# Moving fill work between score halves, warm-up matmuls and norms in an attention-plus-MLP kernel

## The chip, the cores and the metric

The kernel runs on one core of a Trainium2 chip. The metric is device microseconds of one execution. TensorE (PE) multiplies matrices into PSUM, VectorE (DVE), ScalarE (ACT) and GpSimd (POOL) do the element-wise work, and SyncE (SP) issues most DMAs. Each engine works through its own instructions in order and waits on semaphores for the others.

## The reference

`S` is 2048 tokens, `D` 512, 32 heads of 16, `F` 1376. `LN` is a layer norm without weights.

```python
xn = LN(x)
q, k, v = split(xn @ wqkv)                   # 32 heads x 16
# every token attends to itself and to 7 earlier tokens, 2 apart
logits = q . k[pos - 2*w] * 16**-0.5, w = 0..7 (masked where pos - 2*w < 0)
s = softmax(logits) @ v, then @ wo
h  = gelu(LN(xn) @ w1)
hs = concat(4 column groups of h, shifted by +1, -1, +2, -2 tokens) @ w2
x1 = xn + hs
g  = silu(x1 + gelu(LN(x1) @ w3) @ w4)
out = x + s * g
```

## The kernel before

Tokens are split into two parities `p` (even and odd), 1024 tokens each, so that a window of 8 tokens 2 apart becomes a window of 8 neighbours. A chunk `c` (0 to 3) is 512 tokens of one parity. The order of the instructions on every engine is written out by hand: the calls from line 684 on emit them in order, each engine takes its own.

Stages, in order:

1. **Start (L159 to L702).** 16 warm-up matmuls on ones (L161). The four 128-token tiles of chunk 0 go one by one through statistics (`ln_first`, L298 to L302: DVE statistics, then a `pow(-0.5)` on POOL), normalisation on DVE (`first_n`, L306), transposes on TensorE and an ACT copy (`first_t`, L314, L315). The first q/k projections (`qk_pair`, L391) follow on halves of the chunk. `mask_cols`, `mask_rows`, `mask_wide`, `mask_turn` and `mask_fill` build a banded penalty that is put beside q and k as extra rows of the contraction.
2. **Projections and first MLP layer (L703 to L763).** For each chunk: statistics (`ln_stats`, L275, L276, and `rsqrt_eps` on POOL, L267, L268), norm (`ln_norm`, L322), transposes (`stage_t`), q/k projection (`qk_pair`, ACT copy L398). The second layer norm of a row that is normalised already is only a factor per token: `ln_again` computes it on POOL (L331, L332, and `rsqrt_eps`), `stage_d` puts it on a diagonal (DVE, L361), `stage_r` spreads it over partitions with one matmul (L368) and an ACT copy (L369), `stage_m` multiplies (DVE, L375). `stage_w1` has 2 x 4 matmuls (L420) and a GELU on ACT. `spread` moves q and k by DMA from SP.
3. **First phase: attends 0 to 8 (even tokens).** 1024 tokens make 9 units (128, then 120 each, 56 at the end). An attend `n` (L836) emits: scores of the first half of the heads (`scores`, L553: 16 small matmuls, 8 into each of two PSUM tiles, tags `s` and `t`, each followed by an exp on ACT, L558); the weighted sum of the attend before (L576); the fill of list `a`; the values of the next unit (L533, copied by DVE, L537); scores of the second half; the fill of list `b`; then the `late` list. The tags `s` and `t` have one buffer each, so a half's matmuls wait for the exps of the half before. Fill is one of `w2_tile` ("w": 4 matmuls L443 and a DVE add L447) and `qk_one` ("q": 4 matmuls L407 and an ACT copy L412). Both and the values take turns in two PSUM banks (tags `w`, `b`). The strings at L776 say which fill goes where.
4. **w3 (L861 on).** 88 x 2 matmuls (L487) with GELUs (L492), and in between the last weighted sum of the first phase, layer norms and loads.
5. **Second phase: attends 9 to 17 (odd tokens).** Here the weighted sum also stands behind the first half, and the values behind the second. The fill is a `w4_tile` (11 matmuls, L507, and a DVE add, L513), split 5 into list `a` and 6 into list `b`; two attends have three `final_tile`s in its place. `gate(t)` follows a finished w4 tile: tanh on ACT (L522) and a product on DVE (L523).
6. **Tail (L893 on).** w4 tiles 8 to 15, each followed by a `final_tile`: 4 matmuls with `wo` (L663), a product on DVE (L671) directly from PSUM or, with `act=True`, after an ACT copy (L670), and an add (L673) on the engine that is passed. The last three tiles (5, 6, 7) have their adds on DVE; the store of the last one is issued by ACT.

Of the kernel before, what the change touches and what calls it, by code (L numbers as in the profile page):

```python
# [9 lines left out]
ALU = mybir.AluOpType  # L10
# [5 lines left out]
def kernel(  # L16
# [14 lines left out]
    nc = tc.nc  # L31
# [8 lines left out]
    NF = (F + P - 1) // P  # L40
    FL = F - (NF - 1) * P
    EPS = 1e-5
# [72 lines left out]
    def psa(name):  # L115
        cnt["p"] += 1
        return pst("sto"[cnt["p"] % 3], name)
# [6 lines left out]
    for c in range(NCH):  # L124
        p, k = c // 2, c % 2
        n = 1 if c == 0 else 2
        for t0 in range(k * TPC, (k + 1) * TPC, n):
            nc.sync.dma_start(
                out=xn[p][:, t0 : t0 + n, :],
# [26 lines left out]
    nhalf = const.tile([P, TPC], F32, name="nhalf")  # L156
    nc.vector.memset(nhalf[:], -0.5)

    wm = psa("warm_ps")  # L159
    for i in range(16):  # L160
        nc.tensor.matmul(  # L161
            wm[:, i % 2, :], lhsT=ones_bf[:], rhs=ones_bf.unsqueeze(1).to_broadcast([P, TPC, P]),
            start=True, stop=True,
        )
# [101 lines left out]
    def rsqrt_eps(dst, var):  # L266
        nc.gpsimd.tensor_scalar(out=dst, in0=var, scalar1=EPS, scalar2=None, op0=ALU.add)  # L267
        nc.gpsimd.tensor_tensor(out=dst, in0=dst, in1=nhalf[:, 0 : dst.shape[-1]], op=ALU.pow)  # L268

    def layer_stats(src, name, lo=0, hi=TPC):  # L270
        n = hi - lo
        st = small.tile([P, n, nc.vector.BN_STATS_DIM], F32, name=name + "s", tag=f"{name}s{n}", bufs=2)
        mv = small.tile([P, n, nc.vector.BN_AGGR_DIM], F32, name=name + "m", tag=f"{name}m{n}", bufs=8 if n == 1 else 4)
        for j in range(n):
            nc.vector.bn_stats(out=st[:, j, :], in_=src[:, lo + j, :])  # L275
            nc.vector.bn_aggr(out=mv[:, j, :], in_=st[:, j, :])  # L276
        rstd = small.tile([P, n], F32, name=name + "r", tag=f"{name}r{n}", bufs=8 if n == 1 else 4)
        rsqrt_eps(rstd, mv[:, :, 1])
        return mv, rstd
# [5 lines left out]
    def ln_stats(c, lo=0, hi=TPC):  # L285
        p, k = c // 2, c % 2
        lns.setdefault(c, []).append((lo, hi, *layer_stats(xn[p][:, k * TPC : (k + 1) * TPC, :], "l1", lo, hi)))
# [3 lines left out]
    def ln_first(j):  # L291
        if not first:
            first["st"] = small.tile([P, TPC, nc.vector.BN_STATS_DIM], F32, name="l0s", tag="l0s", bufs=1)
            first["mv"] = small.tile([P, TPC, nc.vector.BN_AGGR_DIM], F32, name="l0m", tag="l0m", bufs=1)
            first["r"] = small.tile([P, TPC], F32, name="l0r", tag="l0r", bufs=1)
            lns[0] = [(0, TPC, first["mv"], first["r"])]
        st, mv, rstd = first["st"], first["mv"], first["r"]
        nc.vector.bn_stats(out=st[:, j, :], in_=xn[0][:, j, :])  # L298
        nc.vector.bn_aggr(out=mv[:, j, :], in_=st[:, j, :])
        r = rstd[:, j : j + 1]  # L300
        nc.vector.tensor_scalar(out=r, in0=mv[:, j, 1:2], scalar1=EPS, scalar2=None, op0=ALU.add)
        nc.gpsimd.tensor_tensor(out=r, in0=r, in1=nhalf[:, 0:1], op=ALU.pow)  # L302

    def first_n(j):
        mv, rstd = first["mv"], first["r"]
        nc.vector.tensor_scalar(  # L306
            out=xn[0][:, j, :], in0=xn[0][:, j, :], scalar1=mv[:, j, 0:1],
            scalar2=rstd[:, j : j + 1], op0=ALU.subtract, op1=ALU.mult,
        )

    def first_t(j):
        pt = pst("wb"[j % 2], "tr_ps").bitcast(BF16)[:, 0, 0:CH].rearrange("p (a q) -> p a q", a=ND)
        for dt in range(ND):
            nc.tensor.transpose(pt[:, dt, :], xn[0][:, j, dt * P : (dt + 1) * P], ident[:])  # L314
        nc.scalar.copy(out=xnT[0][:, :, j * P : (j + 1) * P], in_=pt)  # L315

    def ln_norm(c):
        p, k = c // 2, c % 2
        x_c = xn[p][:, k * TPC : (k + 1) * TPC, :]
        for lo, hi, mv, rstd in lns[c]:  # L320
            for j in range(lo, hi):
                nc.vector.tensor_scalar(  # L322
                    out=x_c[:, j, :], in0=x_c[:, j, :], scalar1=mv[:, j - lo, 0:1],
                    scalar2=rstd[:, j - lo : j - lo + 1], op0=ALU.subtract, op1=ALU.mult,
                )

    def ln_again(c):
        r2 = small.tile([P, TPC], F32, name="r2", tag="r2")
        for lo, hi, mv, rstd in lns[c]:
            r = r2[:, lo:hi]  # L330
            nc.gpsimd.tensor_tensor(out=r, in0=rstd, in1=rstd, op=ALU.mult)  # L331
            nc.gpsimd.tensor_tensor(out=r, in0=r, in1=mv[:, :, 1], op=ALU.mult)  # L332
        rsqrt_eps(r2, r2)
        r2s[c] = r2

    def stage_t(c, h):
# [29 lines left out]
    def stage_r(c):  # L366
        rp = psb("rrep_ps")
        nc.tensor.matmul(rp, lhsT=ones_bf[:], rhs=dgs.pop(c).rearrange("p j q -> p (j q)"), start=True, stop=True)  # L368
        nc.scalar.copy(out=xn2T[c][:, ND - 1, :], in_=rp)  # L369
# [41 lines left out]
        dst, n0 = qk_dst(p, nt)  # L411
        nc.scalar.copy(out=dst[:, n0, cs], in_=pt)  # L412

    def stage_w1(c, a):
        p, k = c // 2, c % 2
        pt = psa("w1_ps")
        for b in range(2):
            g = 2 * a + b
            for dt in range(ND):
                nc.tensor.matmul(  # L420
                    pt[:, b, :], lhsT=w1_sb[:, dt, g * P : (g + 1) * P], rhs=xn2T[c][:, dt, :],
                    start=(dt == 0), stop=(dt == ND - 1),
                )
        nc.scalar.activation(
            hT[p][:, 2 * a : 2 * a + 2, 1 + k * CH : 1 + (k + 1) * CH], pt, AF.Gelu_apprx_tanh
        )
# [90 lines left out]
    def gate(t):  # L517
        c, jj = t // TPC, t % TPC
        p, i = c // 2, (c % 2) * TPC + jj
        x_i = xn[p][:, i, :]  # L520
        sig = fin.tile([P, D], BF16, name="sig", tag="f")
        nc.scalar.activation(sig, x_i, AF.Tanh, scale=0.5)  # L522
        nc.vector.scalar_tensor_tensor(out=x_i, in0=sig, scalar=1.0, in1=x_i, op0=ALU.add, op1=ALU.mult)  # L523
# [134 lines left out]
    def final_tile(p, i, eng=nc.vector, ps=psb, act=False):  # L658
        pt = ps("wo_ps")
        if ps is psa:  # L660
            pt = pt[:, 0, :]
        for dt in range(ND):
            nc.tensor.matmul(  # L663
                pt, lhsT=oT[p][:, dt, i * P : (i + 1) * P], rhs=wo_sb[:, dt, :],
                start=(dt == 0), stop=(dt == ND - 1),
            )
        cnt["g"] += 1
        sg = at(75 + cnt["g"] % 4, 1, D)[:, 0, :]
        if act:
            nc.scalar.copy(out=sg, in_=pt)  # L670
        nc.vector.tensor_tensor(out=sg, in0=sg if act else pt, in1=xn[p][:, i, :], op=ALU.mult)  # L671
        x_o = xo[p][:, i, :]
        eng.tensor_tensor(out=x_o, in0=sg, in1=x_o, op=ALU.add)  # L673
# [13 lines left out]
    mask_forms(0)  # L687
    first_n(0)
    first_t(0)
    ln_first(2)  # L690
    mask_forms(1)
    first_n(1)
    first_t(1)
    parts = [qk_pair(0, a, 2) for a in range(3)]
    parts[0][0]()
    ln_first(3)
# [43 lines left out]
    ln_stats(3, 0, 2)  # L740
    stage_d(2)
    ln_stats(3, 2, 4)
    ln_again(3)
    ln_norm(3)
    stage_w1(1, 0)
    stage_w1(1, 1)
    stage_r(2)
# [3 lines left out]
    stage_t(3, 1)  # L751
    stage_d(3)
    qk_pair(2, 1)[0]()
    stage_r(3)
    stage_m(3)
    mask_fill(1)
    spread(0, CH, M)
    stage_w1(2, 0)
    stage_w1(2, 1)
    load_w3()  # L760
    stage_w1(3, 0)
# [3 lines left out]
    N1 = NU  # L765
# [7 lines left out]
    w2q = [lambda t=t: w2_and(t) for t in range(S // P)]  # L773
    qkq = [lambda t=t: qk_one(2 + t // 8, t % 8) for t in range(4, 16)]
    for n, (a, b) in enumerate(
        (("www", "qq"), ("w", "qw"), ("w", "qq"), ("w", "qw"), ("w", "qq"), ("w", "qw"), ("w", "qq"), ("w", "qw"), ("w", "w"))  # L776
    ):
        for i, x in enumerate((a, b)):
            for y in x:
                groups[n][i].append((w2q if y == "w" else qkq).pop(0))  # L780
    assert not w2q and not qkq
    late = {n: [] for n in range(2 * NU + 4)}
# [13 lines left out]
    w4s = [w4_tile(t) for t in range(S // P)]  # L796
    fill = {0: (0, 1), 1: (2,), 3: (3,), 4: (4,), 5: (5,), 7: (6,), 8: (7,)}
    rows_of = {2: (0, 1, 2), 6: (3, 4, 5)}
    ready = ()
    for k in range(NU):  # L800
        a, b = groups[N1 + k]
        gates = [lambda t=t: gate(t) for t in ready]
        ready = fill.get(k, ())
        if ready:
            a += gates
            if len(ready) == 2:
                a.append(lambda t=ready[0]: w4s[t](0, NF))
            t = ready[-1]
            a.append(lambda t=t: w4s[t](0, 5))
            b.append(lambda t=t: w4s[t](5, NF))  # L810
        else:
            i0, i1, i2 = rows_of[k]
            a.append(lambda i=i0: final_tile(0, i, nc.gpsimd))
            a.append(lambda i=i1: final_tile(0, i, nc.gpsimd))
            a += gates
            b.append(lambda i=i2: final_tile(0, i, nc.gpsimd))
# [83 lines left out]
    for t in range(8, 16):  # L900
# [5 lines left out]
        if t < 15:  # L906
            p, i = fq.pop(0)
# [4 lines left out]
        if t == 10:  # L912
            normalise_mid(1, 2)
            normalise_rr(1, 2)
    final_tile(1, 5, ps=psa, act=True)
    store(nc.sync, 1, 4)
    gate(15)
    final_tile(1, 6, ps=psa, act=True)
    store(nc.sync, 1, 6, 1)
    final_tile(1, 7, ps=psa)  # L920
    store(nc.scalar, 1, 7, 1)
# [30 lines left out]
```

The softmax here doesn't subtract the row's maximum and nothing guards it: scores larger than these inputs give would overflow.

## Time and profile before

| what | us |
|---|---|
| median of 8 runs | 211.86 (211.37 to 212.21) |
| the profiled execution | 212.0 |
| its span in the profile | 210.0 |
| busy: TensorE | 201.8 |
| busy: DVE | 137.2 |
| busy: ACT | 133.5 |
| busy: POOL | 76.2 |

Times in the profile count from the span's start. A line such as `L507` is a line of the kernel before. The chain of work that ended last goes back from the last instruction to what released it, or to the instruction ahead of it on its engine; each of its rows has a start, a duration and an instruction, `x16` meaning that 16 of them are merged. A timeline row has start, length, engine, line, output<-input and shape, and in brackets the idle time ahead of it and what ended it. The busy share of TensorE counts overlapping matmuls once and includes short waits inside a group, so the distances between starts tell more than the busy time.

### The profile page before, as it was taken

The page shows a single profiled execution, that of the slowest core. Times are in us where ns is not written, and L with a number is a line of the kernel's source. Part 1 is how long each engine was busy: PE and PEld are TensorE (multiplying, and loading weights), DVE is VectorE, ACT ScalarE, POOL GpSimd, SP SyncE. Part 2 cuts the span into 40 slices and gives each one's busy share as a digit, 9 for nine tenths or more (in the row PEclk, how much of TensorE's full clock was granted, in tenths as well). Part 3 has the DMA queues.
Part 4 walks back from the last instruction along what each step waited for, and adds up shares of the span by engine and source line. Part 5 has one row for each costly group of instructions (what it writes and reads, how often), then busy time and mean ns, then how long its engine had stood idle before and what let it go on. Part 6 is the DMA issues. An engine that isn't in the chain of part 4 may idle for free.

```text
span 210.0 us, 5030 instructions
## 1 busy us (share of the span) xinstructions
PE 201.8 (96%) x2023; PEld 98.5 (47%) x2023; DVE 137.2 (65%) x264; ACT 133.5 (64%) x163; POOL 76.2 (36%) x151
## 2 busy tenths in 40 slices
PE   8899999799999999999999999999999999999990
PEld 2575455344444444454444444444544445444440
DVE  4878988436397879597860100258666858779774
ACT  2374877758989898865556555888888775122130
POOL 6869456300032879920164000001850392700000
PEclk9999999999999999999999999999999999999997
DMA  5991067046800587765359894769040042454202
GB/s 140 356 349 60 1 99 102 2 70 100 268 36 2 126 182 110 157 169 109 104 119 227 159 303 94 101 137 327 13 77 3 19 103 40 105 174 120 91 14 100
DMA packets 30574, 25.55 MB, mean 122 GB/s; under 512 B 12488, under 2 KB 28200, under 8 KB 30552
## 3 DMA queue, kind: packets, MB, share of 16 engines
q1 hardware_dynamic: 28360, 21.96, 41.4%
q0 software_dynamic: 2048, 3.15, 9.0%
q8 instruction: 16, 0.26, 0.5%
q10 hardware_dynamic: 144, 0.13, 0.2%
q14 instruction: 6, 0.05, 0.1%
HBM read 12.39 MB, written 4.46 MB: 80 GB/s over the span
## 4 chain that ended last, share of the span: by engine, by line
PE 83%; DVE 8%; POOL 6%; issue 1%; ACT 1%
PE w_ps L507 19%; PE w_ps L487 18%; PE v_ps L533 8%; PE s_ps L553 7%; PE w_ps L443 7%; PE wo_ps L663 6%; PE qk_ps L407 5%; PE o_ps L576 4%; PE w_ps L420 3%; POOL l1r L268 3%; PE warm_ps L161 3%; DVE l1s L275 2%; PE qk_ps L391 1%; DVE arena L322 1%; DVE arena L361 1%
## 5 line engine op out<-in xcount | busy, mean ns | idle before, releaser
L558 ACT ACTIVATE arena<-s_ps 128x960 bf16<-128x960 f32 (+2 forms) x72 | 63.2, 933 | 15.7 <-PE s_ps L553 15.0
L507 PE MATMUL w_ps<-arena 128*128 128x512 bf16 (+1 forms) x164 | 39.1, 380 | 0.0
L492 ACT ACTIVATE arena<-w_ps 128x1024 bf16<-128x1024 f32 x20 | 20.5, 1024 | 15.3 <-PE w_ps L487 15.3
L618 POOL DMA_DIRECT2D arena<-orw x48 | 24.9, 527 | 9.0 <-DVE orw L588 7.9
L487 PEld LDWEIGHTS <-arena 128*128 128x128 bf16 (+1 forms) x176 | 17.5, 100 | 20.2
L507 PEld LDWEIGHTS <-arena 128*128 128x128 bf16 (+1 forms) x176 | 16.4, 98 | 19.6 <-issue 0.4
L673 POOL TENSOR_TENSOR arena<-arena 128x512 bf16<-128x512 bf16 x6 | 7.7, 1302 | 45.8 <-DVE arena L671 45.8
L522 ACT ACTIVATE sig<-arena 128x512 bf16<-128x512 bf16 x16 | 10.0, 630 | 19.0 <-DVE arena L513 19.0
L588 DVE CAST orw<-o_ps 128x960 bf16<-128x960 f32 (+2 forms) x18 | 19.7, 1093 | 2.3 <-PE o_ps L576 2.3
L391 PE MATMUL qk_ps<-arena 128*128 128x512 bf16 (+1 forms) x104 | 18.7, 330 | 1.2 <-ACT arena L315 0.9
L487 PE MATMUL w_ps<-arena 128*128 128x512 bf16 (+1 forms) x88 | 19.5, 379 | 0.0
L487 PE MATMUL w_ps<-arena,arena 128*128 128x512 bf16 (+1 forms) x88 | 19.2, 379 | 0.0
L537 DVE CAST v_aug<-v_ps 128x512 bf16<-128x512 f32 (+1 forms) x18 | 12.4, 689 | 10.0 <-PE v_ps L533 10.0
L553 PEld LDWEIGHTS <-arena 32*128 32x128 bf16 (+1 forms) x576 | 11.5, 94 | 15.6 <-issue 15.2
L533 PE MATMUL v_ps<-wv_sb,arena 128*128 128x512 bf16 (+1 forms) x72 | 18.6, 380 | 0.0
L553 PE MATMUL s_ps<-arena 32*128 32x120 bf16 (+2 forms) x576 | 17.6, 211 | 0.0
L447 DVE TENSOR_TENSOR arena<-w_ps,arena 128x512 bf16<-128x512 f32 x16 | 11.0, 687 | 9.6 <-PE w_ps L443 9.5
L513 DVE TENSOR_TENSOR arena<-w_ps,arena 128x512 bf16<-128x512 f32 x16 | 11.1, 691 | 8.3 <-PE w_ps L507 8.2
L267 POOL TENSOR_SCALAR l3r<-l3m 128x1 f32<-128x1 f32 (+1 forms) x10 | 2.3, 228 | 38.9 <-DVE l3m L276 38.8
L443 PE MATMUL w_ps<-arena 128*128 128x512 bf16 x64 | 16.3, 381 | 0.0
L644 DVE TENSOR_TENSOR arena<-arena,orw 128x1440 bf16<-128x1440 bf16 (+1 forms) x2 | 1.7, 843 | 21.7 <-DMA orw<-rden_d 21.7
L420 PE MATMUL w_ps<-arena 128*128 128x512 bf16 x64 | 14.5, 379 | 0.0
(98 smaller groups left out, 284.4 us busy)
## 6 DMA issues: line engine op xcount, KB each, us to landing
arena<-arena SPq DMA_DIRECT2D x48, 64.0 KB, 2.5
x1n_dram<-arena SPq DMA_DIRECT2D x4, 512.0 KB, 3.4
arena<-in_A_x_dram SPq DMA_DIRECT2D x4, 512.0 KB, 5.9
out_dram<-arena SPq DMA_DIRECT2D x7, 256.0 KB, 2.1
arena<-in_A_x_dram SPq DMA_DIRECT2D x6, 256.0 KB, 7.1
arena<-in_B_w_dram SPq DMA_DIRECT2D x1, 1376.0 KB
arena<-in_B_w_dram SPq DMA_DIRECT2D x1, 1280.0 KB
arena<-in_A_wqkv_dram SPq DMA_DIRECT2D x2, 512.0 KB, 4.7
```

The costliest lines, as they stand in the source:

```text
L391: nc.tensor.matmul(pt[:, b, hh * w : (hh + 1) * w], lhsT=wqk_sb[:, dt, nt * P : (nt + 1) * P], rhs=xnT[p][:, dt, k * CH + hh * w : k * CH ...
L420: nc.tensor.matmul(pt[:, b, :], lhsT=w1_sb[:, dt, g * P : (g + 1) * P], rhs=xn2T[c][:, dt, :], start=(dt == 0), stop=(dt == ND - 1),)
L443: nc.tensor.matmul(pt, lhsT=w2_src(p, g, m0), rhs=w2_sb[:, g, :], start=(g == 0), stop=(g == ND - 1))
L487: nc.tensor.matmul(pt[:fs, ft % 2, :], lhsT=w3_sb[:, dt, ft * P : ft * P + fs], rhs=x1nT[c][:, dt, :], start=(dt == 0), stop=(dt == ND - 1),)
L492: nc.scalar.activation(h3(c, 2 * a, 2), pt, AF.Gelu_apprx_tanh)
L507: nc.tensor.matmul(pt, lhsT=h3(c, ft, 1)[:fs, 0, jj * P : (jj + 1) * P], rhs=w4_sb[:fs, ft, :], start=(ft == 0), stop=(ft == NF - 1),)
L533: nc.tensor.matmul(vp[:nk, :], lhsT=xnT[p][:, dt, k0 : k0 + nk], rhs=wv_sb[:, dt, :], start=(dt == 0), stop=(dt == ND - 1),)
L553: nc.tensor.matmul(st[:nk, b, i * nq : (i + 1) * nq], lhsT=kT[e][r : r + 32, dt, k0 : k0 + nk], rhs=qT[e][r : r + 32, dt, q0 : q0 + nq], s ...
L558: nc.scalar.activation(prv[:nk, 2 * h : 2 * h + 2], st[:nk, :, 0 : 4 * nq], AF.Exp, scale=SCALE)
L588: nc.vector.tensor_copy(out=orw[p][:, :, :, q0 - ra : q0 - ra + nq], in_=op[:, :, 0 : 4 * nq].rearrange("p j (s q) -> p j s q", q=nq),)
L618: nc.gpsimd.dma_start(out=oT[p][DH * hh : DH * (hh + 1), :, ra : ra + rw], in_=orw[p][32 * cg : 32 * cg + DH, jj],)
L663: nc.tensor.matmul(pt, lhsT=oT[p][:, dt, i * P : (i + 1) * P], rhs=wo_sb[:, dt, :], start=(dt == 0), stop=(dt == ND - 1),)
```

## The change

- Warm-up: 13 matmuls instead of 16.
- `first_n(1)` and `first_t(1)` are emitted ahead of `ln_first(2)` and `mask_forms(1)`.
- `ln_again(3)` computes its first five instructions on DVE instead of POOL, after `ln_norm(3)` instead of ahead of it; the `pow` stays on POOL. The other chunks keep POOL.
- `stage_w1(2, 0)` is emitted ahead of `stage_m(3)`, and `stage_r(3)` now lies between its two groups of 4 matmuls.
- First phase: another order of fill. From attend 3 on a projection is in list `a` and two w2 tiles are in list `b`.
- Second phase: w4 tiles are split 6 and 5 instead of 5 and 6, and `gate(0)` goes from list `a` of attend 10 to the late list of attend 9.
- Tail: `final_tile(1, 5)` without the ACT copy and with its add on POOL; the add of `final_tile(1, 6)` on POOL too.

```diff
-    for i in range(16):
+    for i in range(13):
         nc.tensor.matmul(
             wm[:, i % 2, :], lhsT=ones_bf[:], rhs=ones_bf.unsqueeze(1).to_broadcast([P, TPC, P]),
...
     def ln_again(c):
         r2 = small.tile([P, TPC], F32, name="r2", tag="r2")
+        eng = nc.vector if c == 3 else nc.gpsimd
         for lo, hi, mv, rstd in lns[c]:
             r = r2[:, lo:hi]
-            nc.gpsimd.tensor_tensor(out=r, in0=rstd, in1=rstd, op=ALU.mult)
-            nc.gpsimd.tensor_tensor(out=r, in0=r, in1=mv[:, :, 1], op=ALU.mult)
-        rsqrt_eps(r2, r2)
+            eng.tensor_tensor(out=r, in0=rstd, in1=rstd, op=ALU.mult)
+            eng.tensor_tensor(out=r, in0=r, in1=mv[:, :, 1], op=ALU.mult)
+        eng.tensor_scalar(out=r2, in0=r2, scalar1=EPS, scalar2=None, op0=ALU.add)
+        nc.gpsimd.tensor_tensor(out=r2, in0=r2, in1=nhalf, op=ALU.pow)
         r2s[c] = r2
...
-    def stage_w1(c, a):
+    def stage_w1(c, a, mid=None):
         p, k = c // 2, c % 2
         pt = psa("w1_ps")
         for b in range(2):
             g = 2 * a + b
+            if b and mid:
+                mid()
...
     first_t(0)
+    first_n(1)
+    first_t(1)
     ln_first(2)
     mask_forms(1)
-    first_n(1)
-    first_t(1)
...
     ln_stats(3, 2, 4)
+    ln_norm(3)
     ln_again(3)
-    ln_norm(3)
...
     qk_pair(2, 1)[0]()
-    stage_r(3)
+    stage_w1(2, 0, lambda: stage_r(3))
     stage_m(3)
     mask_fill(1)
     spread(0, CH, M)
-    stage_w1(2, 0)
     stage_w1(2, 1)
...
-        (("www", "qq"), ("w", "qw"), ("w", "qq"), ("w", "qw"), ("w", "qq"), ("w", "qw"), ("w", "qq"), ("w", "qw"), ("w", "w"))
+        (("www", "qq"), ("q", "wq"), ("q", "wq"), ("q", "ww"), ("q", "ww"), ("q", "ww"), ("q", "ww"), ("q", "ww"), ("q", "w"))
...
             if len(ready) == 2:
                 a.append(lambda t=ready[0]: w4s[t](0, NF))
+                late[N1 + k].append(lambda t=ready[0]: gate(t))
+                ready = ready[1:]
             t = ready[-1]
-            a.append(lambda t=t: w4s[t](0, 5))
-            b.append(lambda t=t: w4s[t](5, NF))
+            a.append(lambda t=t: w4s[t](0, 6))
+            b.append(lambda t=t: w4s[t](6, NF))
...
-    final_tile(1, 5, ps=psa, act=True)
+    final_tile(1, 5, nc.gpsimd, ps=psa)
     store(nc.sync, 1, 4)
     gate(15)
-    final_tile(1, 6, ps=psa, act=True)
+    final_tile(1, 6, nc.gpsimd, ps=psa, act=True)
     store(nc.sync, 1, 6, 1)
     final_tile(1, 7, ps=psa)
     store(nc.scalar, 1, 7, 1)
```

## Prediction

> **What bounds the kernel.** I read four views of the profile, in this order: the page's engine shares, the chain of work that ended last, the waits, and the timeline of single stretches.
>
> ```profile
> PE 201.8 (96%) x2023; PEld 98.5 (47%) x2023; DVE 137.2 (65%) x264; ACT 133.5 (64%) x163; POOL 76.2 (36%) x151
> ...
> PE 83%; DVE 8%; POOL 6%; issue 1%; ACT 1%
> ```
>
> TensorE is the bound: from 39.34 us to the end of its work near 205 the chain is matmuls only, one directly behind the other. So only three things can shorten the kernel: fewer us before that stretch, less waiting inside it, and a shorter tail behind it. The chain shows each place:
>
> ```profile
> 34.38 0.72 POOL l1r L268
> ...
> 36.01 1.07 POOL r L332
> 37.15 0.24 POOL r L267
> 37.47 1.05 POOL r L268
> 38.54 0.75 DVE arena L361 x4
> 39.34 0.39 PE rrep_ps L368
> 39.73 6.91 PE w_ps L420 x32
> ...
> 158.33 0.34 PE s_ps L553 x16
> 158.67 0.53 PE o_ps L576 x32
> 159.21 1.19 PE w_ps L507 x5
> 160.39 0.62 PE s_ps L553 x16
> 161.01 0.97 PE v_ps L533 x4
> 161.98 1.30 PE w_ps L507 x6
> 163.28 0.34 PE s_ps L553 x16
> ```
>
> Before 39.34 a DVE/POOL chain sets the time; TensorE idles 1.05 us for it, then runs 32 matmuls at 6.91/32 = 0.216 us. Inside the stretch a score group of 16 takes 0.34 us, or 0.62 where its second PSUM tile is still being read by an exp: 0.28 us of hidden wait. The rule comes from the timeline:
>
> ```profile
> 138.39 0.41 PE L553 MATMUL s_ps<-arena 32*128 32x120 bf16 x16
> ...
> 138.86 1.83 ACT L558 ACTIVATE arena<-s_ps 128x960 bf16<-128x960 f32 x2 [0.66 <-ACT arena L558]
> ```
>
> A group starts at T, its two exps start at T + 0.48 and take 1.83. Where the next group is late, its end is about 0.37 after the exps' end (group at 140.48, exps end 140.69, next matmul at 141.06). So a group's end may not come before the last group's start + 2.68. With two groups of 0.34 the work between them must be 2.68 - 0.68 = 2.0 us, else the difference is waited. This holds for the example: 0.53 + 1.19 = 1.72, wait 0.28.
>
> **What the Trainium skill says.** "SBUF — State Buffer", section "Who interferes with whom": a VectorE instruction with two SBUF inputs and a GpSimd instruction that reads SBUF contend for a port pair, and the later one blocks fully. The trace agrees:
>
> ```profile
> 24.05 3.45 POOL L268 TENSOR_TENSOR l1r<-l1r,nhalf 128x4 f32<-128x4 f32 x1
> 24.11 2.49 DVE L239 COPY arena<-arena 128x2048 bf16<-128x2048 bf16 x4
> ...
> 146.31 2.71 POOL L673 TENSOR_TENSOR arena<-arena 128x512 bf16<-128x512 bf16 x2 [33.95 <-DVE arena L671]
> 146.90 1.11 DVE L523 SCALAR_TENSOR_TENSOR arena<-sig,arena 128x512 bf16<-128x512 bf16 x1
> ```
>
> The first pow takes 3.45 instead of 1.05: it ends 0.90 after the copies. L523 takes 1.11 instead of 0.68, because a POOL add (1.15 alone) holds the port until 147.46; L523 ends 0.54 later. "TensorE: Matmul & The Clock Gate", section "What's actually happening": the array runs at half rate until a free-running 3.4 us window was busy. Here warm-up matmuls start 0.43 us apart until 6.14 us and 0.22 apart after.
>
> **Part 1, the start.** Three warm-ups fewer: twelve are over at 6.17 in either case, so the thirteenth ends near 6.4, against 7.05 for all 16. Norm 1 goes ahead of the third statistics and waits for its pow (5.30 + 0.66), so it ends at 6.4 instead of 6.94; the two transposes and ACT copies (1.07) follow, and the first projection starts at 7.95 instead of 8.60. Its weights, landed 4.7 us after their issue at 2.6, are there at 7.3. The price is on DVE: statistics 3 start near 6.4 instead of 5.46, pow 3 goes from 6.73 to 7.5, and behind it mask_forms(1) (0.88) delays pow 4 to 8.9: norm 3 ends 9.9 instead of 9.2. TensorE loses some 0.1 for each of tiles 2 and 3. mask_cols comes at 11.2 instead of 11.66, POOL's mask rows at 11.7 instead of 12.18, and the pow behind L375 ends near 15.8 instead of 16.15. The chain is ahead by 0.35 (0.1 to 0.6); nothing in DVE's and POOL's order changes from there to the last norm at 35.87.
>
> **Part 2, second norm on DVE, w1 around the rrep.** Five tiny DVE instructions replace the POOL ones. DVE shows no 128x2 tensor_tensor; the nearest, the 128x1 tensor_scalar L301, takes 0.15. I take 0.14 each in sequence, 0.7 (bounds 0.4 and 0.9). Behind them on DVE is queued L375 (1.22), which starts before POOL has seen the semaphore, so the pow is blocked again. Sum: 35.87 - 0.35 + 0.7 + 1.22 - 0.08 (overlap) = 37.36; + 0.90 pow = 38.26; + 0.04 + 0.74 (four L361) + 0.06 = 39.10 for the rrep, against 39.34. The larger piece is that four of the 32 w1 matmuls, 0.86 us, now run ahead of it: TensorE has finished its projections by 37.9, and stage_m(2) by 37.4. The 12 w1 matmuls behind the rrep (2.6 us) cover its ACT copy (0.59) and stage_m(3) (1.23). ACT and SP order is kept (the spread's DMAs wait for mask_fill as before). Gain 0.24 + 0.86 = 1.1 us (0.4 to 1.5). What is late next: the rrep itself, TensorE still idling some 0.3.
>
> **Part 3, first phase (attends 0 to 8).** The same 12 projections and 16 w2 tiles lie between the groups, one fill behind the first half and two behind the second. So the gaps stay 0.53 + 0.97 + 0.86 = 2.36 and 0.97 + 0.86 = 1.83, and the second still waits 0.17 (0.51 instead of 0.34), seven times. The copies (0.60 each) go from behind the second exps to between them, where ACT was idle (0.5 to 1.0 us before the second exps); the exps they delayed, those of the first half, had the gap of 2.36 as cover already. DVE now gets two w2 adds in a row: per attend 3 x 0.69 + 1.16 + 1.7 (two statistics) = 4.9 of 5.05 us, which just fits. I take zero; bounds -0.3 and +0.8.
>
> **Part 4, second phase.** With the fill split 6/5 the gaps are 0.53 + 1.19 + 0.22 = 1.94 and 0.97 + 1.30 - 0.22 = 2.05. The waits of the fill attends behind the first gap are, from the chain, 0.25 + 0.12 + 0.28 + 0.28 + 0.14 = 1.07; 0.06 stays in three of them: 0.9 gained. gate(0)'s tanh (0.63) moved behind attend 9's exps lets the next second exps start earlier, which frees the 0.15 behind them; it may cost 0.06 at the group just after it. Its DVE part (L523) also moves earlier, ahead of work that is not waited for. Attends with final tiles keep their waits. Gain 0.95 (0.6 to 1.1).
>
> **Part 5, the tail.** Before, the last DVE add ends at 207.28:
>
> ```profile
> 203.33 0.59 ACT arena L670
> ...
> 206.86 0.42 DVE arena L673
> ```
>
> Dropping tile 5's ACT copy lets tanh 15 run at 203.25 and L523 at 203.94. But the adds of tiles 5 and 6 become POOL adds of 1.15. Add 5 is asked for at 204.10, blocked by L523 until 204.63, and ends at 205.68. L671 of tile 6 (two SBUF inputs, ready at 204.82) is blocked until then and ends at 206.0; add 6 takes the port from 206.06 to 207.22; the last DVE add, ready at 206.62, is blocked to 207.22 and ends at 207.5. Loss 0.25. If nothing blocked, DVE would end at 206.3: a gain of 1.0. I take the loss, since the 146.31 rows show blocking; both ends stay in the range.
>
> **Sum.** -1.1 + 0 - 0.95 + 0.25 = -1.8 us. The profiled execution took 212.0 (span 210.0 and 2.0 around it), so it would take 210.2; the median of the runs shown, 211.86, becomes 210.1.
>
> **Rivals.** (a) The tail pays after all: adds and DVE pass each other; 1.0 less, near 209.0. For it: no such collision with a plain tensor_tensor on DVE is in the rows. Chance 0.2. (b) The front pays little: the five DVE instructions and a worse block of the pow eat the four matmuls' lead, or first-phase adds arrive late; 0.8 more, 210.9. Chance 0.15. (c) Slower: the clock. The warm-up now ends 0.2 us after the switch that the trace shows. If the window falls later, the array idles between transposes and first projection in a window that is not full, and stays at half rate for the next 3.4 us. Price: 24 projection matmuls of 0.109 at 0.213, 2.5 us on the path to mask_cols; 212.6. It decides from some 17 such matmuls at half rate. Against it: 5.3 us of warm-up remain. Chance 0.1. (d) Gains and losses cancel, 211.7: 0.05. The forecast has 0.5, with its own range 209.5 to 210.7.
>
> **Chances.** 0.2%, 0.42 us, is about what a measurement tells from no change. Faster: 0.5 + 0.2 + 0.13 = 0.83; same 0.07; slower 0.10. The range 208.8 to 211.1 takes in (a) and (b) and leaves out (c) and (d).
>
> **What would show it.** Right: the first L391 near 7.95; the rrep of chunk 3 near 39.1 with four w1 matmuls before it; first-phase groups still 0.51 and 0.34; second-phase groups near 0.4; POOL adds of over 1.5 us in the tail and a last add near 207.5 less 2 us. Wrong: a half-rate stretch behind 6.4 us, gaps before w2 matmuls in the first phase, or POOL and DVE overlapping freely in the tail.

## The result, and the profile after

| kernel | us, median | runs |
|---|---|---|
| before | 211.88 (211.26 to 212.44) | 32 |
| after | 213.33 (213.13 to 213.43) | 11 |
| after / before | 1.007, 95% interval 1.006 to 1.0081 | |

The changed kernel is slower by 1.45 us. Its profiled execution took 213.17 us, with a span of 211.1 (before: 212.0 and 210.0). From here on, lines are those of the changed kernel: from L424 to L680 four more than before (w1 is L424, scores L557, w4 L511), from L345 to L414 two more (the rrep is L370, the q copy L414), with `ln_again` at L332 to L335.

The page of the changed kernel, engine shares and, below, the shares of the chain that ended last:

```profile
PE 199.7 (95%) x2020; PEld 96.9 (46%) x2020; DVE 137.5 (65%) x267; ACT 133.9 (63%) x162; POOL 78.0 (37%) x148
...
PE 74%; DVE 11%; POOL 6%; ACT 3%; issue 2%; DMA 1%; POOLq 0%
```

TensorE is busy 2.1 us less, and yet the span is 1.1 longer. So the loss must lie where TensorE doesn't work. The chain of the changed kernel through the start of the long stretch (start, duration, instruction):

```profile
34.37 0.73 DVE arena L322 x2
...
35.67 0.18 DVE r L334
35.85 0.07 issue
35.92 1.92 POOL r L335
37.84 0.02 issue
37.86 0.76 DVE arena L363 x4
38.62 0.05 issue
38.67 0.39 PE rrep_ps L370
39.06 6.04 PE w_ps L424 x28
45.10 0.86 PE v_ps L537 x4
45.96 0.35 PE s_ps L557 x16
```

28 w1 matmuls stand behind the rrep instead of 32, and the first scores start at 45.9 instead of 47.4. The same view in the second phase:

```profile
157.47 1.40 PE w_ps L511 x6
158.87 0.34 PE s_ps L557 x16
159.22 0.97 PE v_ps L537 x4
160.18 1.08 PE w_ps L511 x5
161.26 0.34 PE s_ps L557 x16
```

The group behind the first gap takes 0.34, where the corresponding one took 0.62. TensorE's last matmul ends at 202.87 instead of 205.02, and the last DVE add at 205.27 instead of 207.28. Up to there the kernel is 2.0 us ahead. From the last DVE add to the end of the span it took 2.7 us before, and takes 5.8 now. What lies there is the program's last line, with a DRAIN in each engine's queue ahead of the semaphores by which the engines meet at the end. Its view gives, per engine queue, operation and count, then the shortest, median and longest duration in ns, and the first and last start in us. Changed kernel:

```profile
L952 POOLq DRAIN  x3: 40/102/6512, 203.8 to 210.8; - x3
L952 SPq DRAIN  x3: 7/7/13, 208.3 to 210.6; - x3
```

Kernel before:

```profile
L947 POOLq DRAIN  x3: 40/102/6472, 182.4 to 209.7; - x3
L947 SPq DRAIN  x3: 7/7/12, 209.1 to 209.5; - x3
```

Both programs end with a DRAIN of 6.5 us on POOL (the first of its three). Before, POOL's last instruction was a DMA at 183.1, and the DRAIN ran from 182.4 to 188.9 beside TensorE's work: SP waits for the last store, which landed at 209.06, and was the last to reach the end. Now POOL's last instruction is an add that ends at 204.99; the DRAIN runs to 210.3, and SP, ready at 208.3, waits for it. SP is itself some 1.1 us late in this execution, since the last store took 2.86 us from issue to landing and not the 1.74 to 1.82 of every other profile here; the DRAIN ends later than that in either case, so the store doesn't set the end.

### The profile page after: what moved, and what is told of

Its sections match the earlier page's. It is cut to its first block, busy times and chain, and to the rows that moved or that the text cites. A ratio compares the mean times of both kernels' runs of the same rounds, so it can differ in the third digit from the quotient of the medians.

```text
span 211.1 us, 5023 instructions
## 1 busy us (share of the span) xinstructions
PE 199.7 (95%) x2020; PEld 96.9 (46%) x2020; DVE 137.5 (65%) x267; ACT 133.9 (63%) x162; POOL 78.0 (37%) x148
## 3 DMA queue, kind: packets, MB, share of 16 engines
q0 software_dynamic: 2048, 3.15, 8.6%
## 4 chain that ended last, share of the span: by engine, by line
PE 74%; DVE 11%; POOL 6%; ACT 3%; issue 2%; DMA 1%; POOLq 0%
PE w_ps L511 19%; PE w_ps L491 18%; PE v_ps L537 7%; PE w_ps L447 7%; PE s_ps L557 6%; PE wo_ps L667 6%; PE o_ps L580 4%; PE qk_ps L409 4%; DVE l1s L275 3%; POOL l1r L268 3%; PE w_ps L424 3%; ACT arena L562 2%; DVE arena L322 1%; DVE arena L363 1%; DMA arena<-in_A_x_dram 1%
## 5 line engine op out<-in xcount | busy, mean ns | idle before, releaser
L511 PE MATMUL w_ps<-arena 128*128 128x512 bf16 (+1 forms) x164 | 39.1, 380 | 0.0
L677 POOL TENSOR_TENSOR arena<-arena 128x512 bf16<-128x512 bf16 x8 | 10.4, 1304 | 66.4 <-DVE arena L675 66.4
L511 PEld LDWEIGHTS <-arena 128*128 128x128 bf16 (+1 forms) x176 | 16.4, 98 | 19.6 <-issue 0.4
L557 PEld LDWEIGHTS <-arena 32*128 32x128 bf16 (+1 forms) x576 | 10.8, 94 | 15.6 <-issue 15.5
L557 PE MATMUL s_ps<-arena 32*128 32x120 bf16 (+2 forms) x576 | 16.8, 211 | 0.1
L517 DVE TENSOR_TENSOR arena<-w_ps,arena 128x512 bf16<-128x512 f32 x16 | 11.1, 692 | 8.7 <-PE w_ps L511 8.6
L447 PE MATMUL w_ps<-arena 128*128 128x512 bf16 x64 | 15.4, 380 | 0.1
L424 PE MATMUL w_ps<-arena 128*128 128x512 bf16 x64 | 14.6, 379 | 0.0
L393 PEld LDWEIGHTS <-arena 128*128 128x128 bf16 x104 | 9.9, 98 | 7.6 <-issue 0.9
```

Of the source, the lines that this page charges most:

```text
L393: nc.tensor.matmul(pt[:, b, hh * w : (hh + 1) * w], lhsT=wqk_sb[:, dt, nt * P : (nt + 1) * P], rhs=xnT[p][:, dt, k * CH + hh * w : k * CH ...
L424: nc.tensor.matmul(pt[:, b, :], lhsT=w1_sb[:, dt, g * P : (g + 1) * P], rhs=xn2T[c][:, dt, :], start=(dt == 0), stop=(dt == ND - 1),)
L447: nc.tensor.matmul(pt, lhsT=w2_src(p, g, m0), rhs=w2_sb[:, g, :], start=(g == 0), stop=(g == ND - 1))
L511: nc.tensor.matmul(pt, lhsT=h3(c, ft, 1)[:fs, 0, jj * P : (jj + 1) * P], rhs=w4_sb[:fs, ft, :], start=(ft == 0), stop=(ft == NF - 1),)
L557: nc.tensor.matmul(st[:nk, b, i * nq : (i + 1) * nq], lhsT=kT[e][r : r + 32, dt, k0 : k0 + nk], rhs=qT[e][r : r + 32, dt, q0 : q0 + nq], s ...
```

## The experiments

The runs came in three groups, each on one chip with its own runs of the kernel before (medians 211.76, 211.42 and 211.58). "After" and "before" in an edit name the kernel that it starts from.

**1. The tail undone.** After, with

```diff
-    final_tile(1, 5, nc.gpsimd, ps=psa)
+    final_tile(1, 5, ps=psa, act=True)
...
-    final_tile(1, 6, nc.gpsimd, ps=psa, act=True)
+    final_tile(1, 6, ps=psa, act=True)
```

> The changed kernel with the tail of the kernel before (both last POOL adds back on DVE, tile 5 with its ACT copy). Theory D (the loss is POOL's closing DRAIN, which runs 6.5 us from the last POOL instruction and is exposed only because the two last adds are on POOL): POOL is done some 20 us before the end, the span ends 2.7 us after the last DVE add as before, so 202.87 + 2.26 + 2.70 = 207.8 us of span and 209.9 us. Rival R1 (the stores at the end are slow, 2.86 us from issue to landing instead of 1.75): at most 1.1 us comes back, 212.2 us. Rival R2 (the gains in the front and the second phase are not real in the timed runs, for instance because of the shorter warm-up): 213.2 us or more.

Measured: 209.78 (209.68 to 210.1), ratio 0.9911 (0.9892 to 0.9929), span 207.9. Against the changed kernel, two lines are worth 3.5 us by the medians (213.33) and 3.4 by the ratios. The program's last line in this kernel:

```profile
L952 POOLq DRAIN  x3: 40/102/6758, 180.3 to 207.6; - x3
```

The DRAIN is as long, but starts at 180.3. The rest of the change is faster than before by 1.9 us. Of the expectation's explanations only D fits: slow stores (R1) allowed 212.2 at best, and gains that aren't real (R2) 213.2 or more.

**2. The new tail alone.** Before, with those two lines the other way round.

> The kernel before with the new tail alone. D: the last POOL add ends near 207.1, the DRAIN 5.3 us later, the span 0.8 after that: 213.3 us of span, 215.3 us. R1: 211.9 + 1.1 = 213.0 us at most. R2: within 0.3 us of the kernel before, 211.9 us.

Measured: 215.13 (214.82 to 215.4), ratio 1.016 (1.014 to 1.018): 3.4 us more, the same price without any other part, where R1 allowed at most 213.0. POOL's timeline and then the program's last line in this kernel:

```profile
203.80 1.47 POOL L673 TENSOR_TENSOR arena<-arena 128x512 bf16<-128x512 bf16 x1 [21.07 <-DVE arena L671]
205.63 1.15 POOL L673 TENSOR_TENSOR arena<-arena 128x512 bf16<-128x512 bf16 x1 [0.36 <-DVE arena L671]
```

```profile
L947 POOLq DRAIN  x3: 40/102/6510, 205.6 to 212.6; - x3
```

**3. One tiny POOL instruction.** The tail of before keeps its adds on DVE; POOL only gets a copy of one column, whose result nothing uses, behind the add of tile 5. Before, with

```diff
     final_tile(1, 5, ps=psa, act=True)
+    tiny = small.tile([P, 1], BF16, name="tiny", tag="tiny", bufs=1)
+    nc.gpsimd.tensor_copy(out=tiny, in_=xo[1][:, 5, 0:1])
```

> The kernel before, plus one copy of a single column on POOL that waits for the last-but-two DVE add (near 204.9 us). It does no useful work. D, if the DRAIN counts from the last POOL instruction whatever its size: DRAIN to 210.4 to 211.5, span 211.2 to 212.2, 213.2 to 214.2 us. D', if the DRAIN waits for the large adds themselves (their writes): no change, 211.9 us. R1 and R2: 211.9 us.

Measured: 213.17 (212.99 to 213.47), ratio 1.007 (1.0053 to 1.0087). POOL's timeline, then the last line:

```profile
204.59 0.58 POOL L917 COPY tiny<-arena 128x1 bf16<-128x1 bf16 x1 [21.81 <-DVE arena L673]
```

```profile
L949 POOLq DRAIN  x3: 40/102/5933, 204.6 to 211.0; - x3
```

The DRAIN starts with the 0.58 us copy and ends at 210.5. Counted from the end of POOL's last instruction it ends 5.33 us later here (205.17 to 210.50), in run 2 (206.78 to 212.11) and in the changed kernel (204.99 to 210.32). So neither the adds as such nor their contention with DVE are needed: one small POOL instruction this late is enough to set the end.

**4. The first phase's order undone too.** Run 1, with

```diff
-        (("www", "qq"), ("q", "wq"), ("q", "wq"), ("q", "ww"), ("q", "ww"), ("q", "ww"), ("q", "ww"), ("q", "ww"), ("q", "w"))
+        (("www", "qq"), ("w", "qw"), ("w", "qq"), ("w", "qw"), ("w", "qq"), ("w", "qw"), ("w", "qq"), ("w", "qw"), ("w", "w"))
```

What is left are the edits ahead of the first phase and the 6/5 split of w4.

> The changed kernel with the tail and with the first-phase order of fill of the kernel before. If the new order costs 0.3 us as the two traces say (first phase 48.14 instead of 47.83 us): 0.3 us less than the run with only the tail undone, 209.6 us with D. If the new order is worth something in itself: 0.3 us or more above that run.

Measured: 209.46 (209.33 to 209.51), ratio 0.9892 (0.9874 to 0.9909): 0.32 faster than run 1, on the same chip and with no overlap of the two ranges. The new order of fill is a small loss.

**5. The values split.** A try at the 0.17 us that the first phase's second groups wait: move one values matmul (0.22) to behind the second half's scores, where the next gap has it to spare. Run 6, with

```diff
+        part(0, ND - 1 if split else ND)
+        return (va, lambda: part(ND - 1, ND)) if split else va
...
         prs.append(scores(p, u, 1))
+        if rest:
+            rest()
```

> The front and the second phase of the change, the first-phase order of before, the last adds on DVE, tile 5's product directly from PSUM, and one thing new: in the first phase the last of the four values matmuls goes behind the scores of the second half. The gaps become 2.36 - 0.22 = 2.14 and 1.83 + 0.22 = 2.05. If the rule holds that two groups need 2.0 us between them, the waits of 0.17 in attends 2 to 8 go: 1.0 to 1.2 us less than the run with the tail of the next kernel of this call, 207.9 us. If the wait is not set by the gap but by something else that reads PSUM at that time, no change: 209.1 us.

Measured: 211.36 (211.21 to 211.91), ratio 0.9989 (0.998 to 0.9999): 2.2 slower than run 6, a miss. The timeline of this kernel in one attend:

```profile
60.58 1.15 DVE L597 CAST orw<-o_ps 128x960 bf16<-128x960 f32 x1
61.65 0.68 DVE L544 CAST v_aug<-v_ps 128x512 bf16<-128x512 f32 x1
62.38 1.02 PE L409 MATMUL qk_ps<-arena 128*128 128x512 bf16 x4 [0.61 <-DVE v_aug L544]
63.34 0.41 PE L562 MATMUL s_ps<-arena 32*128 32x120 bf16 x16
```

The score groups no longer wait, but the fill does: its PSUM bank is freed by the values' copy, which now stands behind the 1.15 us `orw` copy on DVE. PE idles 0.61. The waits of TensorE for this copy in the whole kernel (total in us, times, longest):

```profile
PE qk_ps L409 <- DVE v_aug L544: 1.3, 3, 0.6
PE w_ps L447 <- DVE v_aug L544: 0.8, 3, 0.3
```

Together they are 2.1 us, about what this run lost.

**6. The tail without copy or POOL.** Run 4, with the add of tile 5 on DVE and its product taken directly from PSUM:

```diff
-    final_tile(1, 5, ps=psa, act=True)
+    final_tile(1, 5, ps=psa)
```

> The run with tail and first-phase order undone (209.46 us), but tile 5's product comes directly from PSUM without ACT's copy, all adds on DVE. DVE's last seven operations of the tail then follow each other from 203.3 - 2.2 on: 0.33 us less, 209.1 us, if the port that POOL adds and DVE share was all that made the new tail longer for DVE. If dropping the copy itself costs (the PSUM read of 0.68 instead of 0.42 on DVE): 209.5 to 209.7 us.

Measured: 209.16 (209.0 to 209.49), ratio 0.9882 (0.9859 to 0.9904). The median is 0.3 below that of run 4, which was on another chip, and the intervals of the ratios overlap: dropping the ACT copy does no harm, and more than that isn't settled.

**7. The front alone.** Before, with the four edits ahead of the first phase (warm-up, first norm, `ln_again`, w1 around the rrep).

```diff
+    ln_norm(3)
     ln_again(3)
-    ln_norm(3)
...
-    stage_r(3)
+    stage_w1(2, 0, lambda: stage_r(3))
```

> The kernel before with the four edits of the front alone (13 warm-ups, second norm ahead of third statistics, second layer norm of chunk 3 on DVE, w1 around the rrep). The prediction's sum: 1.1 us less, 210.7 us. From the two profiles (first scores at 45.89 instead of 47.43): 1.5 us less, 210.3 us. If the warm-up's cut costs on average what it saved in this one profile: 211.3 us or more.

Measured: 210.44 (210.42 to 210.78), ratio 0.9947 (0.9926 to 0.9967), which is 1.1 us by the ratio (0.7 to 1.6) and 1.0 by the medians.

**8. The w4 split alone.** Before, with

```diff
-            a.append(lambda t=t: w4s[t](0, 5))
-            b.append(lambda t=t: w4s[t](5, NF))
+            a.append(lambda t=t: w4s[t](0, 6))
+            b.append(lambda t=t: w4s[t](6, NF))
```

and the new place of `gate(0)`.

> The kernel before with the second phase's edit alone (6/5 and the moved gate). The prediction: 0.95 us less, 210.8 us. If the waits only move (to the values' group or to the w4 tiles behind): 211.6 us or more.

Measured: 210.47 (210.25 to 211.37), ratio 0.9949 (0.9935 to 0.9963), 1.1 us by the ratio and 1.0 by the medians. By the ratios, runs 7 and 8 add up to run 4 within their intervals (1.1 + 1.1 against 2.3).

**9. The values split, copies in the other order.** Run 5, with the values' copy ahead of the `orw` copy:

```diff
-        if out and n < N1:
-            out()
         prs.append(scores(p, u, 1))
         if rest:
             rest()
+        if out and n < N1:
+            out()
```

> The run with split values, with DVE's copy of the weighted sum (1.15 us) behind its copy of the values instead of ahead of it. If the new wait there is the PSUM bank that the values' copy frees, it shrinks from 0.4 to 0.8 us to about 0.1 per attend while the score groups keep their 0.34: 208.8 us, a little under the run with the tail without copy (209.16). If the split itself costs (one more switch of TensorE, another order of banks): 211 us as with the split before.

Measured: 208.73 (208.67 to 209.09), ratio 0.9869 (0.985 to 0.9888). The median is the lowest of all, but this ratio's interval overlaps that of run 6. Its timeline in the attend that was shown for run 5:

```profile
60.61 0.69 DVE L544 CAST v_aug<-v_ps 128x512 bf16<-128x512 f32 x1 [0.28 <-PE v_ps L539]
61.22 1.15 DVE L597 CAST orw<-o_ps 128x960 bf16<-128x960 f32 x1
...
62.31 0.41 PE L562 MATMUL s_ps<-arena 32*128 32x120 bf16 x16
```

The second fill has no wait left, and by the ratios 2.5 us of run 5's time are gone: that confirms the bank as the cause of the miss. The 2.0 us rule for the gaps is borne out in part. The second groups of the fill attends take 0.34 now, but three first groups still take 0.43 to 0.45. Each of them follows an attend with two projections, whose two ACT copies delay the exps (in the attend shown they start at 62.99, 0.68 after their group and not 0.48), so the 2.0 us hold only where nothing delays the exps. And from the first scores to w3 this profile takes 45.34 us, that of run 6 45.73: 0.4 less, where run 5 had hoped for 1.0 to 1.2. Part of the rest is the split itself, since the values matmul that was moved takes 0.32 in the chain, not 0.22.

**10. Sixteen warm-ups.** Run 6, with `range(16)` for `range(13)` at L160.

> The run with the tail without copy, with 16 warm-ups again instead of 13. If the clock switches at another time in each execution (3.9 to 7.1 us in the traces so far) and the 13 matmuls are over by 6.6 us at the latest, 16 cost nothing where it switches early and 0.6 us where it switches at 6 us or later; on the chain only part of it arrives: median 209.2 to 209.6 us, spread wider. If the shorter warm-up is what made the front faster: 209.8 us or more. If the shorter warm-up cost something (array back at half rate): under 209.1 us.

Measured: 209.34 (209.26 to 209.66), ratio 0.9893 (0.9873 to 0.9913); run 6 had 209.16, with overlapping ranges and on another chip. Inconclusive: what the shorter warm-up is worth is not shown.

**11. No DMA issued by POOL.** After, with both kinds of POOL's DMAs issued by SP:

```diff
-                nc.gpsimd.dma_start(
+                nc.sync.dma_start(
                     out=oT[p]
...
-        late[4 + w].append(lambda w=w: spread(1, 0, CUT, nc.gpsimd, (w,)))
+        late[4 + w].append(lambda w=w: spread(1, 0, CUT, nc.sync, (w,)))
```

> The changed kernel with every DMA that POOL issued (packs and the spreads of the odd tokens) issued by SP instead; the two last adds stay on POOL. If POOL's closing DRAIN belongs to the DMAs that it issued: the DRAIN is short (under 1 us), the span ends 0.8 us behind SP's last wait, some 2 us less than the changed kernel, unless SP's longer queue costs it elsewhere. If it belongs to any last POOL instruction: it again ends 5.3 us behind the last add.

One execution: 222.33, span 220.4. It is slower for another reason, which the waits show:

```profile
PE w_ps L491 <- DMA arena<-x1n_dram: 9.9, 1, 9.9
```

w3 waits 9.9 us for a load, and TensorE's last matmul is at 215.3. That the added DMAs ahead of this load in SP's queue hold it up is likely, but not shown. What the run was made for is its end. POOL's last instruction in the timeline, the program's last line, and the only large DMA queue that is left:

```profile
216.29 1.15 POOL L677 TENSOR_TENSOR arena<-arena 128x512 bf16<-128x512 bf16 x1 [0.36 <-DVE arena L675]
```

```profile
L952 POOLq DRAIN  x3: 45/78/1259, 216.3 to 220.2; - x3
```

```profile
q1 hardware_dynamic: 33480, 25.11, 47.8%
```

The add has the same shape and place, but the DRAIN takes 1.26 us and ends 0.07 after the add. So the 5.3 us go with a program whose POOL has issued DMAs; in the changed kernel the last of these was issued at 181, 24 us before. This rests on one execution, and how many such DMAs it takes wasn't tried.

**12. The start alone.** Before, with 13 warm-ups and the first norm moved, without `ln_again` and w1.

> The kernel before with the first two edits alone: 13 warm-ups and the second norm ahead of the third statistics. The prediction's part 1: 0.35 us less on the chain, 211.2 us against 211.5. From the traces of the changed kernel (last norm of the chain at 35.10 to 35.63 instead of 35.87): 0.25 to 0.75 us less, 210.8 to 211.3 us. Then the rest of the front's gain (1.0 us of the 210.44 run) belongs to the four w1 matmuls ahead of the rrep.

Measured: 211.53 (211.24 to 212.0), ratio 0.9997 (0.9984 to 1.0011): no change, though the interval reaches down to the 0.35 that was forecast. The chain of this kernel:

```profile
37.94 0.75 DVE arena L361 x4
38.69 0.05 issue
38.74 0.39 PE rrep_ps L368
```

In this execution the rrep is at 38.74 instead of 39.34, the first projection starts at 7.95, exactly as part 1 had it, and yet the median doesn't move. So a single profile's start can't be compared to a few tenths here.

## Why the prediction was wrong, step by step

It forecast 1.8 us faster; 1.45 slower came. Nearly the whole miss, 3.1 us in the profile, lies in one place.

**Part 5, the step that failed.** Its sum ended with the last DVE add ("the last DVE add ... is blocked to 207.22 and ends at 207.5"), as if the rest of the program then followed at the same distance for any tail. What POOL still does at the program's end was put at nothing, without a reason, although the edit gave POOL its last instruction 22 us later than before. The part that was counted held. DVE's and POOL's timelines in the changed kernel:

```profile
202.66 1.10 DVE L675 TENSOR_TENSOR arena<-arena 128x512 bf16<-128x512 bf16 x1 [0.19 <-ACT arena L674]
203.69 0.68 DVE L675 TENSOR_TENSOR arena<-wo_ps,arena 128x512 bf16<-128x512 f32 x1
204.40 0.87 DVE L677 TENSOR_TENSOR arena<-arena 128x512 bf16<-128x512 bf16 x1
```

```profile
202.01 1.47 POOL L677 TENSOR_TENSOR arena<-arena 128x512 bf16<-128x512 bf16 x1 [21.06 <-DVE arena L675]
203.84 1.15 POOL L677 TENSOR_TENSOR arena<-arena 128x512 bf16<-128x512 bf16 x1 [0.36 <-DVE arena L675]
```

Shifted by the 2.15 us that TensorE is ahead, the POOL adds end at 205.63 and 207.14 and the last DVE add at 207.42, where 205.68, 207.22 and 207.5 were forecast. The two-input product of 0.42 took 1.10, blocked by POOL's add; the add of 1.15 took 1.47. This agrees with the Trainium skill, "SBUF — State Buffer", "Who interferes with whom": the later one of such a pair waits fully. So rival (a), adds that pass DVE freely, is out. (Of the prediction's two examples only the second is such a pair; L239 in the first is a copy with one input.) The distance from the last matmul to the last add grew by 0.14 (2.26 to 2.40; forecast 0.25). Behind it came the DRAIN: 5.33 us after POOL's last instruction, and 0.8 more for the engines to meet (1.1 in run 2). SP is ready at 208.3, so in this execution the DRAIN decides once POOL's last instruction ends later than 208.3 - 5.3 = 203.0; with a last store as fast as in the other profiles it would be about 201.9. Runs 1 and 2 show the price, 3.5 and 3.4 us; that of the copy alone, in run 3, is smaller (1.4), since it ends at 205.17 and not, as the add in run 2, at 206.78. Run 11 shows what it goes with.

**Part 1.** Forecast 0.35 on the chain; run 12 shows 0 in the median, with 0.34 at the edge of its interval. The first projection did start early, at 7.32 (forecast 7.95), but the clock's switch in the profiles of these kernels lies anywhere between 3.9 and 7.1 us, and with 13 warm-ups the first projection goes with it, from 7.32 to 8.36. In run 12, where the switch comes at 6.2 as it did before, it starts at 7.95, so this step of the sum held; why the median doesn't show it stays open. The Trainium skill, "TensorE: Matmul & The Clock Gate", "What's actually happening", speaks of a free-running window, which fits this spread, though the ±500 ns that it gives are less than the 3.2 us seen here. Rival (c), the clock staying at half rate behind a late switch, wasn't seen, not even where the switch came at 7.1, after the last warm-up.

**Part 2.** Right in mechanism and size. From the norm's end to the rrep it takes 3.56 us (35.10 to 38.67), against 3.47 before and 3.58 in the forecast: moving `ln_again` to DVE costs 0.1, since the pow is blocked by L377 as forecast (1.92 instead of 1.05). The gain is the four w1 matmuls: from the rrep to the first scores 7.23 instead of 8.09, so 0.86, as forecast. Parts 1 and 2 together were put at 1.1 (the 0.24 in part 2's sum has part 1's 0.35 in it), and run 7 measured 1.1. With nothing from part 1 in run 12, the profile's 0.76 for part 2 alone leaves 0.3 unexplained; run 7's interval (0.7 to 1.6) takes in both sums, so the close agreement is partly luck.

**Part 3.** Forecast zero, with bounds of -0.3 and +0.8; run 1 less run 4 is +0.32, and the profile has +0.31 from the first scores to w3. Attends 4 to 7 keep 0.51 and 0.34, as forecast. What was overlooked is in the first attends, where two q copies stand ahead of the exps, as before, but the fill ahead of the w2 tile is now a projection, so that its bank is freed by ACT and no longer by a DVE add. The chain of the changed kernel:

```profile
52.26 0.97 ACT arena L414 x2
53.23 1.74 ACT arena L562 x2
54.97 0.49 ACT arena L414
55.45 0.04 issue
55.50 1.02 PE w_ps L447 x4
```

A w2 tile waits for a PSUM bank that a q copy frees, which stands behind the delayed exps: ACT sets the chain from 51.2 to 55.5. At 60.82 an exp starts some 0.3 late (0.80 after its group's start instead of 0.48) with no cause that the profile shows; that part stays open.

**Part 4.** Right: forecast 0.95, 0.92 in the profile (45.69 to 44.77 for the second phase), 1.1 in run 8 (0.8 to 1.4).

Parts 1 to 4 were forecast at 2.05 together; run 4, which leaves out part 3, gives 2.3. No rival named what happened: the one on the slower side was put on the clock, and not on the end of the program.

## What to carry to other kernels

A sum along the chain ends when every engine has ended, not with the last result: of each engine that gets a later last instruction, look up in the profile what its queue still does behind it, and what hides that now. An engine that has been free for long (POOL here, 22 us) is not free of cost at the end; with the tail's adds left on DVE and the first phase's old order, the front, the w4 split and the two moves of run 9 give 208.73. When matmuls are moved, ask which copy frees the PSUM bank of the next one, and what stands before that copy on its engine.

## What the runs showed of the hardware

- POOL's closing DRAIN ends 5.3 us after POOL's last instruction where POOL has issued DMAs (5.33 in each of three kernels; 5.7 to 6.2 where that instruction is itself a DMA), though the last was issued 22 to 24 us earlier, and 0.07 us after it in the kernel without any. The Trainium skill, "DMA: Bandwidth & Descriptors", "SWDGE vs HWDGE vs iDMA", says that DMAs issued from GpSimd have their descriptors computed by software on it; the traces agree so far that such a kernel has a queue `software_dynamic` (2048 packets in the changed kernel) and run 11 has none. What the DRAIN does in that time no run shows.
- The clock's first switch to full rate came between 3.9 and 7.1 us after the span's start in the profiles of the 14 kernels, with 13 or 16 warm-ups of the same kind.
